# One step more of weight decoding among the attention steps of a fused attention and MoE kernel

## The chip, the cores and the metric

One core of one Trainium2 chip. The metric is the device time of one execution in microseconds (us); of several runs the median is given. TensorE multiplies, VectorE and ScalarE work element by element, GpSimd does some of that too, and SyncE's queue (SP) issues the transfers.

## The reference, cut to what matters

```python
# q, k, v: (2, 12, 448, 64); 896 tokens of 768
scores = scale * np.matmul(q, k.transpose(0, 1, 3, 2))      # causal mask, softmax
attn = np.exp(scores) / (np.sum(...) + 1e-09)
x = np.matmul(attn, v)                                      # -> (896, 768)
h = np.maximum(np.maximum(x @ w1, x @ w2), x @ w3)          # 768 x 768 each
x = h @ w_out                                               # 768 x 768
g = s * np.maximum(x @ w_in, 0.0) ** 2 + b                  # 768 x 2048
out = g @ w_out2                                            # 2048 x 768
```

## The kernel before

Attention comes first: 24 heads in 12 pairs, in a hand-written pipeline of steps t = 0 to 27. `ORDER` lists for even and odd steps the operations by two-letter names: S scores, R maxima (L252), E exponentials (L260), T transposes of the probabilities (L309) and V their copies (L397), PV the product with v (L324), N1 and N2 the reciprocals of the sums (L401, L404), RT, RV, Q1, Q2 the way of these out: a transpose (L282), a copy `rows` (L285), a store `rcd` to DRAM (L288) and a spread load `rb` (L293). XM divides (L339, result `xf`), XO and XL split that into the x tiles on GpSimd. M works at the first MoE product (the early product), and W runs a step of weight decoding at the steps t that `STEPS` names.

The weights come as 56 raw tiles of 768 KB, 64-bit words that have to be turned into 32-bit floats, then split into a high and a low part, since a matmul pass keeps only part of a float's digits. So each product is three passes: `whi` with the high part of the activations, `whi` with their low part, and `wlo` with the high part. A tile's decoding has four stages, one a step, and a new tile enters at every second call (`now[0] % 2`):

1. enter: ScalarE `wa` (L133) and `wr` (L134) read the raw tile;
2. clamps: VectorE L137, L140;
3. rounding: VectorE L146 and L151; between them `fetch_w` puts the load of another raw tile on SP's queue;
4. split: ScalarE `whi` (L156), VectorE `wlo` (L86).

So every call runs either the half "split of one tile, clamps of the next" or the half "rounding of one tile, enter of the next". In the MoE part there is one call per product. A product here is 18 matmuls of 448 columns (one 128-wide tile of weights, one half of the tokens); products are numbered from 0, the early one not counted: 0 to 34 use w1, w2, w3, 35 to 46 w_out, 47 to 78 w_in (two products per weight tile). The output stage (L559) follows: 2 halves of 16 calls of 21 matmuls of 384 columns, accumulated in seven PSUM tiles `m` for the seven blocks of tokens. `m` has eight buffers (banks) in all, for products and accumulators alike.

The evacuation of product k is queued with `after` and runs in the calls that follow: for w_in the Relu (L544) at call k + 1; at k + 2 VectorE's L533, which reads the bank for the last time, and on ScalarE L536 and L539 (`g`); at k + 3 VectorE's L86 (`g`, the low part). A call runs due evacuations first, the older ahead of the younger, and decoding behind them. The engines wait for each other only where data or buffers demand it; each works off its own queue in order.

```python
        for fns in [s.pop(0) for s in stages]:
            for fn in fns:
                fn()
        if not (enter and raws) or now[0] % 2:
            return
...
            acc = [ps.tile([128, 512], F32, tag="m", name="m") for _ in range(NTT)]
```

Of the kernel before, what the change touches and what calls it, by code (L numbers as in the profile page):

```python
# [27 lines left out]
)  # L28


FETCH = 18
STEPS = (20, 21, 23, 24, 25, 27)
EARLY = {24: 2, 25: 2, 26: 1, 27: 1}


# [8 lines left out]
def kernel(  # L44
# [55 lines left out]
    def begin(enter=True):  # L100
        for _, fn in sorted(due.pop(now[0], []), key=lambda e: e[0]):
            fn()
        decode(enter)
        now[0] += 1
# [5 lines left out]
    def fetch_w():  # L110
        if w_src:
            src = w_src.pop(0)
            raw = wr_p.tile([128, DM], I64, tag="wraw", name="wraw")
            nc.sync.dma_start(out=raw, in_=src)
            raws.append(raw)
# [54 lines left out]
    def attention():  # L170
        with ExitStack() as c2:
# [208 lines left out]
            def emit(t):  # L380
# [47 lines left out]
                if t in EARLY:  # L428
                    ops["M"] = lambda: [next(first, None) for _ in range(EARLY[t])]
                ops["W"] = lambda: [begin() for at in STEPS if at == t]  # L430
                for n in ORDER[h]:
# [3 lines left out]
            for t in range(n_heads + 4):  # L435
                emit(t)
                if t == FETCH:
                    fetch_w()
# [187 lines left out]
```

## Time and profile before

| | |
|---|---|
| median of 3 runs | 561.89 us (560.36 to 564.05) |
| the profiled execution | 564.4 us, of it 562.4 from first to last instruction |
| TensorE busy | 540.3 us, 96% |
| VectorE busy | 349.3 us, 62% |
| ScalarE busy | 293.1 us, 52% |
| GpSimd busy | 47.6 us, 8% |
| mean granted clock of TensorE | 0.994 of full |

Busy shares are averages over stages with different limits, and overlapping matmuls count as busy; where TensorE is not full, one has to look at the stage. Times on the timeline are counted from the first instruction. `PEclk` in the windows is the granted clock of TensorE as a part of full speed.

### The profile page before, as it was taken

What the parts mean: (1) busy time and instruction counts of PE and PEld (TensorE: products, weight loads), DVE (VectorE), ACT (ScalarE), POOL (GpSimd) and SP (SyncE); (2) the same over time, 40 slices, a digit from 0 to 9 for tenths busy, and PEclk for the clock granted to TensorE, in tenths of its full rate; (3) what the DMA queues carried; (4) which work ended last, traced back from release to release, by engine and by line L of the source; (5) the groups of instructions that cost most, each with busy time, mean ns of one, the idle gap of its engine ahead of it and who ended that gap; (6) DMA issues with size and microseconds to landing.
All of it is one profiled execution on the core that took longest, in us unless ns stands there. A gap on an engine that the chain in (4) does not pass through costs nothing.

```text
span 562.4 us, 7508 instructions
## 1 busy us (share of the span) xinstructions
PE 540.3 (96%) x2789; PEld 459.5 (82%) x2789; DVE 349.3 (62%) x653; ACT 293.1 (52%) x574; POOL 47.6 (8%) x43
## 2 busy tenths in 40 slices
PE   8999999989999999999999999888989799999997
PEld 4566665648999999999999997776768799999997
DVE  3555656676666676767666566575756677537501
ACT  2677777774335344344444575757666564334201
POOL 3125343222000000000000000000000000000000
PEclk9999999989999999999999999999999899999999
DMA  8768697523333333332323331313223144344102
GB/s 216 202 175 235 177 226 202 158 90 114 112 113 112 113 113 112 111 107 86 117 99 108 106 106 64 112 57 112 65 104 111 59 146 145 113 148 165 57 0 99
DMA packets 21108, 68.43 MB, mean 122 GB/s; under 512 B 3088, under 2 KB 9744, under 8 KB 21072
## 3 DMA queue, kind: packets, MB, share of 16 engines
q1 hardware_dynamic: 21072, 67.95, 38.6%
q8 instruction: 22, 0.36, 0.3%
q14 instruction: 14, 0.11, 0.1%
HBM read 55.05 MB, written 2.80 MB: 103 GB/s over the span
## 4 chain that ended last, share of the span: by engine, by line
PE 73%; ACT 16%; DVE 9%; issue 2%; ACTq 0%
PE m L453 31%; PE m L559 20%; PE s L244 9%; PE t L309 5%; PE o L324 5%; ACT r L536 4%; ACT g L539 3%; DVE wlo L86 3%; ACT r L544 2%; ACT whi L156 2%; ACT wa L133 2%; ACT wr L134 2%; PE warm L354 2%; DVE g L86 2%; DVE r L533 2%
## 5 line engine op out<-in xcount | busy, mean ns | idle before, releaser
L453 PE MATMUL m<-x,whi 128*128 128x448 f32 x816 | 233.8, 368 | 9.4 <-ACT whi L156 8.8
L453 PEld LDWEIGHTS m<-x,whi 128*128 128x128 f32 x816 | 152.5, 188 | 27.0 <-ACT whi L156 12.8
L453 PE MATMUL m<-x,wlo 128*128 128x448 f32 x408 | 150.8, 370 | 3.5 <-DVE wlo L86 3.5
L86 DVE TENSOR_TENSOR wlo<-wa,whi 128x768 fp32r<-128x768 f32 x56 | 53.6, 958 | 105.8 <-ACT whi L156 105.8
L559 PE MATMUL m<-whi,g 128*128 128x384 f32 x448 | 115.3, 337 | 2.6 <-DVE r L533 1.8
L453 PEld LDWEIGHTS m<-x,wlo 128*128 128x128 f32 x408 | 76.9, 188 | 14.0 <-DVE wlo L86 7.9
L559 PEld LDWEIGHTS m<-whi,g 128*128 128x128 f32 x448 | 81.9, 190 | 3.3 <-DVE r L533 2.2
L559 PE MATMUL m<-wlo,g 128*128 128x384 f32 x224 | 75.6, 338 | 0.5 <-DVE wlo L86 0.5
L133 ACT ACTIVATE wa<-wraw 128x768 f32<-128x768 f32 x56 | 51.0, 911 | 31.2 <-DMA wraw<-in_w_dram 25.2
L252 DVE CUSTOM_DVE_ANT_0 s<-s,mask 112x224 f32<-112x224 f32 (+1 forms) x96 | 43.7, 456 | 32.9 <-PE s L244 32.0
L156 ACT CAST whi<-wa 128x768 fp32r<-128x768 f32 x56 | 46.6, 831 | 32.1 <-PE m L559 16.4
L260 ACT ACTIVATE P<-s,mx 112x224 f32<-112x224 f32 (+1 forms) x96 | 46.8, 493 | 23.6 <-DVE mx L252 19.9
L151 DVE CUSTOM_DVE_ANT_0 wa<-wa,wr 128x1536 uint16<-128x1536 uint16 x56 | 54.7, 977 | 1.9
L146 DVE SCALAR_TENSOR_TENSOR wa<-wraw,wa 128x768 int32<-128x768 int32 x56 | 53.4, 954 | 0.5
L536 ACT ACTIVATE r<-r,sb 128x448 f32<-128x448 f32 x32 | 24.3, 758 | 51.1 <-DVE r L533 51.1
L134 ACT ACTIVATE wr<-wraw 128x768 int32<-128x768 uint32 x56 | 50.3, 899 | 0.0
L559 PEld LDWEIGHTS m<-wlo,g 128*128 128x128 f32 x224 | 42.5, 190 | 0.8 <-DVE wlo L86 0.8
L453 PE MATMUL m<-h,whi 128*128 128x448 f32 x144 | 40.9, 365 | 0.0
L244 PE MATMUL s<-HL 64*112 64x224 f32 (+3 forms) x112 | 39.4, 387 | 0.0
L397 ACT COPY PT<-t 112x336 f32<-112x336 f32 (+1 forms) x72 | 31.4, 476 | 11.1 <-PE t L309 11.1
L140 DVE TENSOR_SCALAR wa<-wa 128x768 int32<-128x768 int32 x56 | 33.0, 590 | 1.9
L309 PE MATMUL t<-ident,P 112*112 112x112 f32 x240 | 32.8, 268 | 0.1
(48 smaller groups left out, 486.7 us busy)
## 6 DMA issues: line engine op xcount, KB each, us to landing
wraw<-in_w_dram SPq DMA_DIRECT2D x56, 768.0 KB
QK<-HL SPq DMA_DIRECT2D x44, 224.0 KB
R<-in_qk_dram SPq DMA_DIRECT2D x11, 448.0 KB
V<-in_v_dram SPq DMA_DIRECT2D x12, 224.0 KB
rb<-rcd SPq DMA_DIRECT2D x24, 112.0 KB
out_dram<-o SPq DMA_DIRECT2D x14, 192.0 KB
R<-in_qk_dram SPq DMA_DIRECT2D x2, 224.0 KB
rcd<-rows SPq DMA_DIRECT2D x12, 3.5 KB
```

What stands on the lines that cost most here:

```text
L86: eng.tensor_tensor(out=lo, in0=full, in1=hi.bitcast(F32), op=ALU.subtract)
L133: nc.scalar.activation(out=f, in_=high.bitcast(F32), func=ACTF.Abs)
L134: nc.scalar.activation(out=r, in_=low.bitcast(U32), func=ACTF.Copy, scale=2.0 ** -29)
L146: nc.vector.scalar_tensor_tensor(out=a, in0=high, scalar=-0x40000000, in1=a, op0=ALU.bitwise_and, op1=ALU.bitwise_or,)
L151: nc.vector.tensor_tensor(out=a, in0=a, in1=r, op=ALU.add)
L156: nc.scalar.copy(out=hi, in_=f)
L244: nc.tensor.matmul(ps[:, o:o + n], lhsT, rhs, start=(m == 0), stop=(m == len(terms) - 1))
L260: nc.scalar.activation(out=s_t["P"][:, poff[i]:poff[i] + n], in_=ps[:, o:o + n], func=ACTF.Exp, bias=s_t["mx"][:, i:i + 1], scale=-1.0, ac ...
L309: nc.tensor.transpose(ps[0:CH, o:o + CH], head[t]["P"][:, a:a + CH], ident[0:CH, 0:CH])
L453: nc.tensor.matmul(p, wt[w][:, ws], cols(act[i], a, b), start=(i == 0 and n == 0), stop=(i == len(act) - 1 and n == 2),)
L536: nc.scalar.activation(out=r, in_=r, func=ACTF.Identity, scale=sb[:, 0:1], bias=sb[:, 1:2])
L559: nc.tensor.matmul(acc[t][:, 0:EH], gt[f][:, a, ts], w[:, ws], start=(f == 0 and n == 0), stop=(f == KG - 1 and n == 2),)
```

## The change

```diff
-FETCH = 18
-STEPS = (20, 21, 23, 24, 25, 27)
+FETCH = 17
+STEPS = (19, 20, 21, 23, 24, 25, 27)
 EARLY = {24: 2, 25: 2, 26: 1, 27: 1}
```

The first two raw tiles are requested behind attention step 17 in place of 18, and there are seven calls of the decoding among the attention steps in place of six. All later calls follow, so each stage of each tile is queued one call earlier, and in the MoE part the two halves change places between even and odd calls. What the attention steps run:

| step | before | now |
|---|---|---|
| 19 | | enter 0 |
| 20 | enter 0 | clamps 0 |
| 21 | clamps 0 | rounding 0, enter 1 |
| 23 | rounding 0, enter 1 | split 0, clamps 1 |
| 24 | split 0, clamps 1 | rounding 1, enter 2 |
| 25 | rounding 1, enter 2 | split 1, clamps 2 |
| 27 | split 1, clamps 2 | rounding 2, enter 3 |

VectorE, end of attention step 23 and step 24, before (`s,mx` are the maxima, `su` the sums, `rows` their copy):

```order
L252 ISA s,mx<-s,mask 112x448
L252 ISA mx 112x1
L146 SCALAR_TENSOR_TENSOR wa<-wraw,wa 128x768
L151 ISA wa<-wa,wr 128x1536
L401 TENSOR_SCALAR su<-su 112x8
L404 RECIPROCAL su<-su 112x8
L285 COPY rows<-t 8x112
L86 TENSOR_TENSOR wlo<-wa,whi 128x768
L137 TENSOR_SCALAR wa<-wa 128x768
L140 TENSOR_SCALAR wa<-wa 128x768
```

and with the change:

```order
L252 ISA s,mx<-s,mask 112x448
L252 ISA mx 112x1
L86 TENSOR_TENSOR wlo<-wa,whi 128x768
L137 TENSOR_SCALAR wa<-wa 128x768
L140 TENSOR_SCALAR wa<-wa 128x768
L401 TENSOR_SCALAR su<-su 112x8
L404 RECIPROCAL su<-su 112x8
L285 COPY rows<-t 8x112
L146 SCALAR_TENSOR_TENSOR wa<-wraw,wa 128x768
L151 ISA wa<-wa,wr 128x1536
```

The split and the clamps now stand ahead of the reciprocals, and the rounding behind the copy of the sums.

VectorE, from the last evacuation of w_out (`x_2857`, an x tile) into the first of w_in, before:

```order
L86 TENSOR_TENSOR x_2857<-m,x_2857 128x448
L146 SCALAR_TENSOR_TENSOR wa<-wraw,wa 128x768
L151 ISA wa<-wa,wr 128x1536
L533 SCALAR_TENSOR_TENSOR r<-m,r 128x448
L86 TENSOR_TENSOR wlo<-wa,whi 128x768
L137 TENSOR_SCALAR wa<-wa 128x768
L140 TENSOR_SCALAR wa<-wa 128x768
L86 TENSOR_TENSOR g<-r,g 128x448
L533 SCALAR_TENSOR_TENSOR r<-m,r 128x448
```

and with the change (the same tile has another number):

```order
L86 TENSOR_TENSOR x_2863<-m,x_2863 128x448
L86 TENSOR_TENSOR wlo<-wa,whi 128x768
L137 TENSOR_SCALAR wa<-wa 128x768
L140 TENSOR_SCALAR wa<-wa 128x768
L533 SCALAR_TENSOR_TENSOR r<-m,r 128x448
L146 SCALAR_TENSOR_TENSOR wa<-wraw,wa 128x768
L151 ISA wa<-wa,wr 128x1536
L86 TENSOR_TENSOR g<-r,g 128x448
L533 SCALAR_TENSOR_TENSOR r<-m,r 128x448
```

The first L533 (product 47) now stands behind the split and the clamps, the second (product 48) behind the rounding; so it goes on for all odd and even products.

SP's queue, from attention step 22 on (`rcd` and `rb` carry the sums, `wraw` is a raw weight tile), as one piece of the difference:

```order
-L288 DMA rcd<-rows 8x112
-L293 DMA rb<-rcd 64x448 x2
 L114 DMA wraw<-in_w_dram 128x768
 L288 DMA rcd<-rows 8x112
 L293 DMA rb<-rcd 64x448 x2
-L114 DMA wraw<-in_w_dram 128x768 x49
+L288 DMA rcd<-rows 8x112
+L114 DMA wraw<-in_w_dram 128x768
+L293 DMA rb<-rcd 64x448 x2
+L114 DMA wraw<-in_w_dram 128x768 x48
```

A load of a raw tile now stands between the last store of sums and the last spread load.

## Rows read from the trace of the kernel before

**Rows 1.** Windows; engines' busy us, granted clock, DMA share, GB/s.

```profile
131.50:303.20 171.70, 171.69 (x847) 159.16 (x848) 118.14 (x166) 75.31 (x105) 1.34 (x1) 1.00 0.32 108
...
345.00:437.00 92.00, 80.87 (x371) 67.72 (x369) 59.54 (x91) 59.73 (x95) 0.00 (x0) 1.00 0.27 92
```

**Rows 2.** Waits from 303 to 444 us: total, times, longest.

```profile
ACT r L536 <- DVE r L533: 47.9, 16, 3.2
...
PE m L453 <- ACT whi L156: 7.7, 10, 0.8
...
ACT r L544 <- PE m L453: 2.4, 1, 2.4
...
PE m L559 <- DVE r L533: 1.8, 1, 1.8
```

**Rows 3.** Timelines, ScalarE, then VectorE, at the end of w_in.

```profile
436.29 0.54 ACT L544 ACTIVATE r<-m 128x448 f32<-128x448 f32 x1
436.73 0.82 ACT L156 CAST whi<-wa 128x768 fp32r<-128x768 f32 x1
...
434.01 0.62 DVE L533 SCALAR_TENSOR_TENSOR r<-m,r 128x448 f32<-128x448 f32 x1
437.58 0.96 DVE L86 TENSOR_TENSOR wlo<-wa,whi 128x768 fp32r<-128x768 f32 x1 [2.94 <-ACT whi L156]
438.45 0.55 DVE L137 TENSOR_SCALAR wa<-wa 128x768 f32<-128x768 f32 x1
439.04 0.56 DVE L140 TENSOR_SCALAR wa<-wa 128x768 int32<-128x768 int32 x1
439.51 0.62 DVE L86 TENSOR_TENSOR g<-r,g 128x448 fp32r<-128x448 f32 x1
440.05 0.62 DVE L533 SCALAR_TENSOR_TENSOR r<-m,r 128x448 f32<-128x448 f32 x1
...
442.98 0.62 DVE L533 SCALAR_TENSOR_TENSOR r<-m,r 128x448 f32<-128x448 f32 x1
```

**Rows 4.** Timelines, ScalarE and VectorE, at the start of w_in.

```profile
306.92 0.55 ACT L544 ACTIVATE r<-m 128x448 f32<-128x448 f32 x1 [2.38 <-PE m L453]
...
308.90 0.62 DVE L533 SCALAR_TENSOR_TENSOR r<-m,r 128x448 f32<-128x448 f32 x1
...
317.51 0.62 DVE L533 SCALAR_TENSOR_TENSOR r<-m,r 128x448 f32<-128x448 f32 x1
```

**Rows 5.** Timeline of TensorE at the start of the output stage.

```profile
437.60 0.45 PE L559 MATMUL m<-whi,g 128*128 128x384 f32 x1 [0.79 <-ACT whi L156]
...
443.65 0.44 PE L559 MATMUL m<-whi,g 128*128 128x384 f32 x1 [1.85 <-DVE r L533]
```

**Rows 6.** A window just behind that wait.

```profile
444.00:446.00 2.00, 2.00 (x8) 2.00 (x7) 0.00 (x0) 1.97 (x5) 0.00 (x0) 0.50 0.48 194
```

**Rows 7.** The seam, steps 22 to 27: timelines, and one window.

```profile
111.84 0.52 DVE L252 CUSTOM_DVE_ANT_0 s<-s,mask 112x336 f32<-112x336 f32 x1 [0.44 <-PE s L244]
...
118.55 1.78 DVE L151 CUSTOM_DVE_ANT_0 wa<-wa,wr 128x1536 uint16<-128x1536 uint16 x1
...
129.56 0.62 DVE L339 TENSOR_TENSOR xf<-o,rb 128x448 f32<-128x448 f32 x1 [2.61 <-PE o L324]
...
119.38 0.95 ACT L133 ACTIVATE wa<-wraw 128x768 f32<-128x768 f32 x1
...
120.71 0.26 PE L282 MATMUL t<-ident,su 112*8 112x112 f32 x1 [0.86 <-DVE su L404]
...
122.32 0.67 PE L453 MATMUL m<-x,whi 128*128 128x448 f32 x2 [1.07 <-ACT whi L156]
...
125.11 1.66 PE L324 MATMUL o<-PT,V 112*64 112x448 f32 x4
...
131.51 0.68 PE L453 MATMUL m<-x,whi 128*128 128x448 f32 x2 [0.62 <-ACT t L462]
...
124.00:126.00 2.00, 2.00 (x8) 0.81 (x6) 1.97 (x4) 1.04 (x2) 1.05 (x1) 0.50 0.31 115
```

## The prediction

> **What bounds the kernel now.** I read the windows first, then the waits of the stage in which TensorE is not full, then the timelines of that stage's two ends, and last the seam between attention and MoE. The windows [rows 1] split the MoE part: from 131.5 to 303.2 us TensorE is busy 171.69 of 171.70 us, so nothing that ScalarE or VectorE do there is on the path; from 345 to 437 us it is busy 80.87 of 92.00 us. Between lies the start of the 32 products of the second MoE's first matrix (47 to 78 in the numbering above). The waits from 303 to 444 us [rows 2] show what rules there: ScalarE waits 47.9 us for `r L533` on VectorE, TensorE waits 7.7 us for `whi`, but ScalarE waits for TensorE once, 2.4 us, at the very start. From then on ScalarE and VectorE turn a closed loop that TensorE does not enter. A turn is two steps: from one even product's L533 to the odd one's is 442.98 - 440.05 = 2.93 us, from the odd one's at 434.01 to the next even one's 6.04 us, 8.97 us together [rows 3]. TensorE at full clock needs less: 171.7 us hold 847 matmuls, 0.203 us each [rows 1], so 36 take 7.3 us. It runs ahead on its stock of weight tiles, uses that stock up, and then stands at each new tile, ten times [rows 2].
>
> The stage does not end when the last weight tile is ready. The output stage takes seven of the eight banks of `m`, its last one is the bank of product 77, and that bank comes free with product 77's L533. TensorE begins at 437.60 us, gets through six accumulators and then stands 1.85 us, until 443.65, for L533 [rows 5], which VectorE began at 442.98 [rows 3]. From there it is busy to the end. So the end is set by one VectorE instruction, L533 of product 77, and about 119 us of matmuls and output behind it.
>
> **The change part by part.** *Weights one product further ahead.* This moves the waits for weights in the w_in stage, and nothing else there: TensorE's stock lasts one product longer, so I expect about seven waits for `whi` in place of ten. But evacuation of 32 products and all decoding still have to go through the loop up to product 77's L533, and no step of evacuation has moved. TensorE will arrive at the output stage about half a turn (4.5 us) earlier and stand for the banks of products 76 and 77 that much longer: the 1.85 us grow to some 5.5 us at the last bank (6.04 - 0.5 for the accumulator between) and about 2 us at the one before. Worth on the path: 0.
>
> *The decode halves change places in the loop.* Each step now holds the other half of the decoding (the second pair of order fences). Before, product 47 ended, its Relu ran at 306.92 us and L533 followed at 308.90 [rows 4], since the step between had only the rounding half, whose VectorE work was already under way. Now that step holds `whi`, `wlo` and the two clamps, and L533 stands behind them. Step by step with the steady rows [rows 3]: Relu to `whi` 0.44 (436.29 to 436.73), `whi` to `wlo` 0.85, `wlo` to L137 0.87, L137 to L140 0.59, L140 to the next 0.47: 3.22, so L533 of product 47 comes at 310.14 in place of 308.90, +1.24. From product 47 to 49 it took 317.51 - 308.90 = 8.61 [rows 4]; now it is the short gap and the long one, 8.97: +0.36. From 49 to 77 there are 14 full turns either way. Product 77's L533 thus comes **1.60 us later**. It is on the path, with no cover.
>
> *The start of the decoding in the attention steps.* The extra step 19 issues only ScalarE's `wa` and `wr`; the clamps move to step 20, the rounding to 21, `whi`, `wlo` to 23. In step 21 VectorE now runs L146 and L151 where it ran the clamps. Beside GpSimd's work L151 took 1.78 us [rows 7]; the step's two instructions so take 2.8 us. Against that stand the clamps removed from this place, and 0.44 us in which VectorE waited for TensorE afterwards [rows 7]. From below, cost 0 (all cover); from above 0.8, if every step passes it on; I take 0.1, since the chain through the next maxima has slack and TensorE's own queue sets the pace of attention.
>
> *The seam.* Before, VectorE finished L151 and went to N1 and N2 (L401, L404), TensorE's transpose of the sums started at 120.71, and the early product stood 1.07 us for `whi` at 122.32 [rows 7]. Now `whi` takes the place of `wa` on ScalarE, 119.38 us plus the 0.1, and the wait for it is gone. But VectorE has `wlo` and both clamps ahead of N1 and N2 (first pair of fences): `whi` at 119.5, and by the same steps as above 0.85 + 0.87 + 0.59 + 0.47 = 2.78 to L401, some 0.4 for L401 and L404 and the signal: the transpose at 122.7, **2.0 us later** than 120.71. The early product follows it after 0.5 us at 123.2, 0.9 later than 122.32. Its first six matmuls then no longer stand between `whi` and `wlo`; at the half clock that this stretch had (0.50 from 124 to 126 us [rows 7]) they need 6 x 2 x 0.203 = 2.4 us and end at 125.6, where the next product of attention began at 125.11 [rows 7]. **+0.5**, and as much for the first whole MoE product, at 131.51 before [rows 7], the 0.1 included. Bounds: -1.1, if the wait of 1.07 vanishes and the transpose costs nothing, and +2.0, if the transpose's delay goes through whole.
>
> *The transfers.* The two fetches stand one attention step earlier on SP, ahead of a store of sums; a fetch now also stands between the last store of sums and the last `rb`. The last divide (L339) stood 2.61 us for TensorE, not for `rb`, and began at 129.56 [rows 7]; that is the cover. I take 0; past the cover it costs what the `rb` is late.
>
> *TensorE's clock.* After the wait at 443.65 the granted clock is 0.50, that is 1.2 of 2.4 GHz, from 444 to 446 us, with 8 matmuls in 2 us [rows 6]; TensorE had stood three times in the 6 us before. Two us at half clock lose 1.0 us; the drop may outlast the window, so I put one drop at 1.6 us, an estimate. A longer wait may give the same drop again (0) or a second one (+1.6). I take 0, as the drop is already paid for.
>
> Sum: 1.60 + 0.5 = **+2.1 us**. The profiled execution took 564.4 us (span 562.4), 2.5 above the median of the runs; set against its own time the changed kernel would take 566.5, and set against the median of 561.89, **564.0 us**.
>
> **A rule that speaks for the change.** The trace shows ten waits for `whi` in 92 us of the stage [rows 2]. The Trainium skill, Perfetto Trace Analysis, section Optimization Strategy, says to look for the gaps on the engine that should be full, find what they wait for, and make that start sooner; by that rule the sum would be rival A's below, by the rows it is +2.1. The same section takes a gap that repeats as a possible sign of too little SBUF or PSUM. The repeating gaps here end with `whi`, but the one that ends the stage does end with a bank [rows 5], and in that the trace agrees.
>
> **The rivals.** *A, the waits go and nothing takes their place.* The output stage then begins half a turn earlier, 4.5 us, and the seam's 1.1 us go too: 561.89 - 5.6 = 556.3. If the drop of the clock at the output stage goes with the wait, 1.6 more. For it speaks that the wait at the last bank is the smallest of the stage, 1.85 us; against it, that product 77's L533 is two steps behind the weights in VectorE's queue and nothing in the change moves it up. Without the seam's part it is 557.4.
>
> *B, the seam turns into a stall.* VectorE stands for `whi` with N1, N2, the rows copy and the next rounding queued behind it; TensorE waits for N2, and behind it the store of sums, the fetch and `rb`. If the 2.0 us go through whole, the half clock lasts one drop longer (1.6) and `rb` comes 2 us after its cover, the price is 5.6 on top of 1.6: 569.1, slower. It decides when the last `rb` lands after about 131 us, so that the last x tile is late for the first product. Before, the window from 124 to 126 us holds 2 us x 115 GB/s = 230 KB [rows 7], which is `rb`'s two halves of 112 KB: they landed by 126. The transpose's 2 us and a tile of 768 KB ahead, 4 us at the 194 GB/s of the window in which one lands [rows 6], make 132 at the latest; most of that overlaps, so I expect some 130 and no price.
>
> *C, the change doesn't do what it says* can be left out: the rows of both orders show each half moved by one step through the whole MoE part.
>
> **How the numbers follow.** Forecast (the end waits for a bank, +2.1): 0.80; A: 0.10, nearly half of it past 1%; B: 0.10, mostly past 1%. A measurement of this kernel tells about 1% from no change, 5.6 us. The forecast's own bounds: 1.6 - 1.1 = +0.5 to 1.6 + 0.8 + 2.0 + 1.6 = +6.0 at the worst of all; runs differ by about 1.9 us to either side (560.36 to 564.05), so I take 560.5 to 567.5, which leaves out A and B. Faster by over 1%: 0.04; within 1%: 0.87; slower by over 1%: 0.09.
>
> **What would show it.** Right: the wait of L559 for L533 grows from 1.85 to over 4 us; TensorE begins L559 earlier but resumes at 445 or later; waits for `whi` in the stage fall to about seven; L533 of product 77 follows a long gap; the transpose L282 of step 24 waits 2 us longer for L404. Wrong: L559 begins 4 us earlier and runs without such a wait (A), or the first MoE product begins after 134 us (B). The forecast also fails if attention itself stretches: ScalarE's `wa` of step 19 would then wait for its raw tile and hold the exponentials behind it.

## The result and the profile after

| | before | changed |
|---|---|---|
| median | 560.36 us (558.63 to 564.05, 13 runs) | 564.02 us (562.34 to 570.44, 13 runs) |
| the profiled execution | 564.4 us, span 562.4 | 562.34 us, span 560.3 |
| mean granted clock in it | 0.994 | 0.991 |

The ratio is 1.0072 [1.0043, 1.0101]: some 4.0 us (2.4 to 5.7) slower, inside the band of 1%, which the interval's upper end just touches. Ratios, and medians that are split by clock below, leave out executions more than 1.5% above the fastest of their kernel. The forecast of 564.0 us is met, but the profiled executions stand the other way round: the one of the changed kernel is the fastest of its 13 runs, the one of the kernel before was slower than all 13 runs of before. So spans can't be set against each other, and the stages have to be.

**The stage of the 32 products, windows of the changed kernel** (columns as in [rows 1]):

```profile
131.50:303.20 171.70, 171.70 (x849) 159.14 (x848) 116.98 (x166) 75.52 (x108) 0.00 (x0) 1.00 0.32 110
345.00:437.00 92.00, 79.69 (x368) 67.22 (x366) 59.93 (x91) 59.74 (x95) 0.00 (x0) 0.99 0.28 94
```

Up to 303 us TensorE is full as before; in the later stretch it does no more than before, 368 matmuls in 92 us beside 371 [rows 1]. **The waits from 303 to 444 us:**

```profile
ACT r L536 <- DVE r L533: 50.0, 16, 3.2
...
PE m L559 <- DVE r L533: 7.0, 2, 4.8
PE m L453 <- ACT whi L156: 5.6, 7, 0.8
...
ACT r L544 <- PE m L453: 1.5, 1, 1.5
```

Against [rows 2] the waits for weights fell from ten to seven (7.7 to 5.6 us), those of the output stage for a bank rose from 1.8 to 7.0 us, and the loop of ScalarE and VectorE is unbroken. **TensorE at the start of the output stage** shows where the waits went:

```profile
429.04 0.45 PE L559 MATMUL m<-whi,g 128*128 128x384 f32 x1 [0.81 <-ACT whi L156]
...
435.09 0.54 PE L559 MATMUL m<-whi,g 128*128 128x384 f32 x1 [2.14 <-DVE r L533]
...
441.11 0.69 PE L559 MATMUL m<-whi,g 128*128 128x384 f32 x1 [4.83 <-DVE r L533]
```

It begins 12.1 us ahead of the last wait's end, before it was 6.05 [rows 5]. **VectorE at both ends of the stage**, with the Relu of product 47 on ScalarE in a fence of its own:

```profile
305.99 0.62 DVE L533 SCALAR_TENSOR_TENSOR r<-m,r 128x448 f32<-128x448 f32 x1
...
314.96 0.62 DVE L533 SCALAR_TENSOR_TENSOR r<-m,r 128x448 f32<-128x448 f32 x1
...
434.42 0.62 DVE L533 SCALAR_TENSOR_TENSOR r<-m,r 128x448 f32<-128x448 f32 x1
437.96 0.96 DVE L86 TENSOR_TENSOR wlo<-wa,whi 128x768 fp32r<-128x768 f32 x1 [2.92 <-ACT whi L156]
...
440.44 0.62 DVE L533 SCALAR_TENSOR_TENSOR r<-m,r 128x448 f32<-128x448 f32 x1
```

```profile
302.75 0.55 ACT L544 ACTIVATE r<-m 128x448 f32<-128x448 f32 x1 [1.50 <-PE m L453]
```

L533 of product 77 (440.44) now follows the long gap of 6.02 us; before it followed the short one of 2.93 [rows 3]. From the Relu of product 47 to it are 137.69 us; before 442.98 - 306.92 = 136.06 [rows 3, 4].

**The clock behind the wait, windows** (as [rows 6]):

```profile
440.00:442.00 2.00, 0.89 (x3) 0.89 (x4) 1.97 (x4) 0.88 (x2) 0.00 (x0) 0.50 0.00 0
442.00:444.00 2.00, 2.00 (x8) 2.00 (x7) 1.98 (x3) 2.00 (x4) 0.00 (x0) 0.50 0.50 135
444.00:446.00 2.00, 2.00 (x9) 2.00 (x8) 0.00 (x0) 1.97 (x4) 0.00 (x0) 0.62 0.65 258
446.00:448.00 2.00, 2.00 (x13) 2.00 (x13) 1.45 (x3) 0.97 (x2) 0.00 (x0) 1.00 0.00 0
```

TensorE, back from the wait at 441.11 us, runs at half clock up to about 445, as before behind its shorter wait.

**The seam, timelines of TensorE, VectorE and ScalarE** (as [rows 7]):

```profile
90.53 0.26 PE L282 MATMUL t<-ident,su 112*8 112x112 f32 x1
...
119.15 0.26 PE L282 MATMUL t<-ident,su 112*8 112x112 f32 x1 [2.83 <-DVE su L404]
...
119.46 0.65 PE L453 MATMUL m<-x,whi 128*128 128x448 f32 x2
...
127.34 0.68 PE L453 MATMUL m<-x,whi 128*128 128x448 f32 x2 [1.39 <-ACT t L462]
```

```profile
116.75 0.96 DVE L86 TENSOR_TENSOR wlo<-wa,whi 128x768 fp32r<-128x768 f32 x1 [2.62 <-ACT whi L156]
...
118.69 0.16 DVE L401 TENSOR_SCALAR su<-su 112x8 f32<-112x8 f32 x1
...
126.07 0.62 DVE L339 TENSOR_TENSOR xf<-o,rb 128x448 f32<-128x448 f32 x1 [0.50 <-PE m L453]
```

```profile
125.18 0.91 ACT L133 ACTIVATE wa<-wraw 128x768 f32<-128x768 f32 x1 [2.75 <-DMA wraw<-in_w_dram]
125.99 0.89 ACT L134 ACTIVATE wr<-wraw 128x768 int32<-128x768 uint32 x1
126.77 0.53 ACT L462 COPY t<-m 128x448 f32<-128x448 f32 x1
```

The first row, the transpose of step 18, runs ahead of the first moved call, and I count from it: it stood at 94.16 us in the profile before, so that execution was 3.6 us late where the change had moved nothing but two requests. In the fourteen profiles taken here that transpose lies anywhere from 90.35 to 94.16 us. The early product no longer waits for `whi`; instead the transpose of step 24 waits 2.83 us for the reciprocals, which stand behind `wlo` and the clamps. New is the end of the seam: `wa` waits 2.75 us for its raw tile, the copy `t`, which frees the early product, is queued behind it, and the first whole product, the one behind the early one, waits 1.39 us for that copy.

Stage by stage, in us from that transpose on. "Again" are two more executions, one of each kernel, from the last part of the experiments:

| | before | before again | changed | changed again |
|---|---|---|---|---|
| to the first whole product | 37.35 | 35.90 | 36.81 | 37.58 |
| from it to the Relu of product 47 | 175.41 | 175.42 | 175.41 | 175.42 |
| from there to L533 of product 77 | 136.06 | 136.13 | 137.69 | 137.74 |
| from there to the end | 119.42 | 117.89 | 119.86 | 119.14 |
| sum | 468.24 | 465.34 | 469.77 | 469.88 |

Against the profile before the change costs 1.5 us, against the second one 4.4. The ratio says 4.0. Which of the two executions of before stands for its runs is therefore the question that the experiments end with.

### The profile page after: what moved, and what is told of

Same layout as the page of the kernel before. It is cut to its first block, busy times and chain, and to the rows that moved or that the text cites. A ratio compares the mean times of both kernels' runs of the same rounds, so it can differ in the third digit from the quotient of the medians.

```text
span 560.3 us, 7507 instructions
## 1 busy us (share of the span) xinstructions
PE 534.4 (95%) x2788; PEld 457.8 (82%) x2789; DVE 348.1 (62%) x653; ACT 292.4 (52%) x574; POOL 47.2 (8%) x43
## 4 chain that ended last, share of the span: by engine, by line
PE 71%; ACT 17%; DVE 8%; issue 2%; DMA 1%; SPq 0%; ACTq 0%
PE m L453 31%; PE m L559 21%; PE s L244 9%; PE t L309 5%; PE o L324 4%; ACT r L536 4%; ACT g L539 3%; DVE wlo L86 3%; ACT r L544 2%; ACT wa L133 2%; ACT wr L134 2%; ACT whi L156 2%; DVE g L86 2%; DVE r L533 2%; DVE wa L137 1%
## 5 line engine op out<-in xcount | busy, mean ns | idle before, releaser
L559 PE MATMUL m<-whi,g 128*128 128x384 f32 x448 | 116.7, 340 | 7.8 <-DVE r L533 7.0
L244 PE MATMUL s<-HL 64*112 64x224 f32 (+3 forms) x112 | 37.6, 364 | 0.2 <-DVE HL L86 0.2
L244 PE MATMUL s<-QK 128*112 128x224 f32 (+1 forms) x88 | 32.7, 371 | 0.0
```

Of the source, the lines that this page charges most:

```text
L244: nc.tensor.matmul(ps[:, o:o + n], lhsT, rhs, start=(m == 0), stop=(m == len(terms) - 1))
L559: nc.tensor.matmul(acc[t][:, 0:EH], gt[f][:, a, ts], w[:, ws], start=(f == 0 and n == 0), stop=(f == KG - 1 and n == 2),)
```

## The experiments

The theory: the end is set by L533 of product 77; the swapped halves make it 1.6 us later, and weights that are ready sooner only lengthen the wait for its bank. The rivals are those of the prediction: the waits for weights were on the path (A), or the loss is the seam's (B). Times are medians; the ratio is to the kernel before, run beside each group.

**1. The loop alone.** The attention steps up to 25 stay as before, and the extra call runs in step 27.

```diff
-STEPS = (20, 21, 23, 24, 25, 27)
+STEPS = (20, 21, 23, 24, 25, 27, 27)
```

> The seventh call stands at the end of attention step 27, so attention up to there is as before and only the MoE part is one call ahead, its halves swapped. Theory (the end waits for the bank of product 77, whose L533 comes 1.6 us later by the swapped halves): +1.6 us against before, up to +3.2 with a longer drop of the clock, and a wait for L533 in the output stage of 4 us or more. Rival A (weights ahead are worth half a turn, and the change lost that in the seam): -4.5 us. Rival B (the loss is the seam's): 0.

567.56 us, 1.006 [1.0027, 1.0093]. From the Relu to L533 of product 77 it took 137.77 us, the changed kernel's figure, and TensorE stood for banks as there:

```profile
441.63 0.44 PE L559 MATMUL m<-whi,g 128*128 128x384 f32 x1 [2.14 <-DVE r L533]
447.66 0.69 PE L559 MATMUL m<-whi,g 128*128 128x384 f32 x1 [5.23 <-DVE r L533]
```

With the weights a product ahead and the first six calls where they were, nothing is won; A falls, and the loss is there without the 2 us at the transposes. But the run is not the loop alone. At the seam the extra call puts `wa` ahead of the copy `t`:

```profile
129.00 1.12 PE L453 MATMUL m<-x,whi 128*128 128x448 f32 x2 [2.37 <-ACT t L462]
```

This first whole product comes 38.65 us behind the transpose of step 18 and starts at half clock (0.50 from 130 to 132 us), and from it to the Relu it took 180.22 us in place of 175.4, most of the difference from matmuls that follow less closely on each other (the last section). So the 1.6 us of the loop are shown by the rows of the stage, not by this ratio.

**2. The seam alone.** All of the change among the attention steps, but the first call of the MoE part leaves its decoding to the next, so that the halves stand as before.

```diff
-        decode(enter)
+        if now[0] != len(STEPS):
+            decode(enter)
```

(with the parity counted by calls of `decode`.)

> The attention part is the changed kernel's, and the decoding of the first MoE call is left out, so the MoE part has the order of before. Theory: the seam is worth -0.5 to +0.5 us against before (in the changed kernel's profile the transpose came 2.07 us later and the first whole product 0.54 us earlier), the wait at the last bank stays at 1.85 us. Rival B: the whole loss of 3.7 us stands here. Rival A: 3.7 + 4.5 = 8 us of loss stand here.

565.36 us, 0.9983 [0.9954, 1.0011]. The wait at the last bank is the one before, 1.81 us, and L533 of product 77 follows the Relu after 136.19 us. The first whole product comes 37.59 us behind the transpose of step 18, as in the changed kernel run again. By the ratio the early attention calls thus cost between 2.6 us less and 0.6 us more than nothing, beside runs of before that had a mean granted clock of 0.994 at the median; B falls as the main loss. The profile holds some 3.4 us between the first whole product and the Relu (178.85 us in place of 175.4) whose cause was not found (the last section).

**3. Two calls more,** from step 18 on, with the requests at step 16: the halves stand as before, the weights are a whole turn ahead.

```diff
-FETCH = 18
-STEPS = (20, 21, 23, 24, 25, 27)
+FETCH = 16
+STEPS = (18, 19, 20, 21, 23, 24, 25, 27)
```

> Eight calls in attention (steps 18 to 27, fetch behind 16): weights two products ahead, the halves in the order of before. Theory: L533 of product 77 as early as before, the loop's +1.6 us gone; the seam has w0 ready two steps early, so -1 to +1 us against before; the output stage begins some 9 us earlier than before and stands that much longer for banks. Rival A: -4.5 us a step, -9 us. Rival B (more decoding in attention costs): +4 us or more.

568.62 us, 1.0054 [1.0019, 1.0089]. The loop did as expected, 136.2 us from the Relu to L533 of product 77, and TensorE stood four times for banks, 8.9 us:

```profile
315.42 0.55 ACT L544 ACTIVATE r<-m 128x448 f32<-128x448 f32 x1 [2.38 <-PE m L453]
```

```profile
451.62 0.62 DVE L533 SCALAR_TENSOR_TENSOR r<-m,r 128x448 f32<-128x448 f32 x1
```

The time did not: about 3 us slower. TensorE's timeline in attention, and two windows:

```profile
97.55 0.33 PE L244 MATMUL s<-QK 128*112 128x224 f32 x1 [1.53 <-DMA QK<-HL]
```

```profile
96.00:102.00 6.00, 4.47 (x21) 2.80 (x20) 3.89 (x11) 2.79 (x10) 1.88 (x2) 0.68 0.53 134
102.00:108.00 6.00, 6.00 (x21) 3.37 (x19) 3.75 (x10) 3.92 (x9) 0.00 (x0) 0.50 0.36 80
```

TensorE waited 1.53 us for a transfer of attention, and the granted clock was 0.50 from 102 to 132 us. This execution is the longest of the 12 and has the lowest mean clock, 0.958; the others had 0.973 to 0.982, so the window shows more than most of them lost. The two requests went out at 84.00 us, ahead of the `QK` requests at 86.22, and the DMA engines were over 0.9 busy from 84 to 96 us; in run 1 the two stand behind the `QK` requests, at 91.26, and TensorE did not wait there. That the one delayed the other fits, but was not tested by itself. A call may so cost through attention what it can't win behind it.

**4 and 5. More room ahead of the bank.** Both kernels with the first half of the output stage in another order: for its first two calls the token blocks 0 to 4 alone, then blocks 5 and 6 of both, so that the last bank is wanted later.

```diff
+LATE = {
+    0: [(0, t) for t in range(5)],
+    1: [(1, t) for t in range(5)] + [(f, t) for t in (5, 6) for f in range(2)],
+}
...
-                for t in range(NTT):
...
+                todo = LATE.get(f) if eh == 0 else None
+                for g, t in todo or [(f, t) for t in range(NTT)]:
+                    part(g, t)
```

> The kernel before, with the output stage's first half in another order: rows of tokens 0 to 4 for the first two calls, then rows 5 and 6 for both. The last bank is wanted 18 matmuls (3.1 us) later. Theory (the bank is what the end waits for): the wait of 1.85 us goes, and with it the drop of the clock: -1.9 to -3.5 us against before. Rival (something else holds the end, for example the next weight tile): 0, with the wait moved.

> The changed kernel with the output stage's first half reordered as in e4: rows of tokens 0 to 4 for two calls, then rows 5 and 6. In the changed kernel TensorE had done 18 matmuls before it stood for the bank of product 77; now it has done 36, 3.1 us more. Theory: the time from L533 of product 77 to the end falls from 119.9 to about 116.5 us (e4: 117.4, before: 119.4), and the weights ahead now show: against before -1 to +1 us, where the changed kernel had +4. Rival (the weight tile is what the output stage waits for): no gain over the changed kernel.

Before with it: 564.59 us, 1.0007 [0.9969, 1.0045]; its wait for L533 is gone, and 0.60 us for the second weight tile stand in its place. The changed kernel with it: 561.36 us, 0.999 [0.9963, 1.0017], beside 1.0055 [1.0023, 1.0087] for the changed kernel in the same group. One wait is left:

```profile
443.68 0.69 PE L562 MATMUL m<-whi,g 128*128 128x384 f32 x1 [4.53 <-DVE r L537]
```

From L533 of product 77 (here L537) to the end it takes 116.0 us in place of 119.86 and 119.14. So wanting the bank later gives the changed kernel some 3 us and the kernel before nothing that the runs show (117.4 us behind that L533 in place of 119.42 and 117.89). Between the two reordered kernels the early weights are worth 1.4 us behind the bank (116.0 and 117.4), just what the swapped halves cost ahead of it: from the Relu to the end it is 253.7 us in both. The times, 0.999 and 1.0007 of before, show no difference either.

**6 and 7. The loop taken apart.** ScalarE's `whi` is queued ahead of the evacuations that are due, `wlo` stays behind them; in the kernel before, and in the changed one.

```diff
     def begin(enter=True):
+        for s in stages:
+            if len(s) == 1:
+                s[0].pop(0)()
         for _, fn in sorted(due.pop(now[0], []), key=lambda e: e[0]):
...
-        stages.append([[clamped], [rounded], [split]])
+        stages.append([[clamped], [rounded], [split_high, split_low]])
```

> The kernel before, with one instruction moved: in the split step ScalarE does whi first, ahead of the due evacuations, and VectorE's wlo stays where it was. Theory (a closed loop of ScalarE and VectorE sets the pace of w_in, each standing 3 us a turn for the other): with whi first, both queues fit into some 7.3 us a turn in place of 8.97, TensorE becomes the bound again, and up to 16 x 1.6 = 26 us go: 535 to 545 us against 560 to 564 before. Rival (the engines' own busy time sets the turn): 0 to -3 us.

> The changed kernel with whi first in the split step. Theory: once the loop is no longer the bound, neither the place of the halves nor the weights one product ahead matter on the path; within 2 us of e9, the rest being the seam. If weights ahead were worth something in themselves: 3 us or more faster than e9. If the swapped halves still cost: 1.6 us slower.

540.35 us, 0.9612 [0.9569, 0.9656], and 539.0 us, 0.9583 [0.9539, 0.9627] (6 and 4 runs): 22 to 23 us faster, and the change worth nothing beyond the spread. The waits from 303 to 444 us of the kernel before with `whi` first, and a window:

```profile
ACT r L543 <- DVE r L540: 23.3, 16, 1.5
```

```profile
345.00:410.00 65.00, 65.00 (x323) 60.22 (x322) 52.93 (x81) 51.31 (x81) 0.00 (x0) 1.00 0.32 110
```

The wait of ScalarE for L533 (here L540) halves from 47.9 us [rows 2], a turn takes 7.32 us in place of 8.97, from one `whi` to the next:

```profile
350.09 0.84 ACT L161 CAST whi<-wa 128x768 fp32r<-128x768 f32 x1
...
357.41 0.84 ACT L161 CAST whi<-wa 128x768 fp32r<-128x768 f32 x1
```

and TensorE is full, with no wait at the output stage. That is the theory's closed loop, shown by breaking it: no more work was done by either engine than before, one instruction of each split stands earlier in one queue.

**8 and 9. Both kernels again.** The changed kernel in the group of 5 to 7, the kernel before in the group of 10 to 12.

> The changed kernel once more, for a second profile beside these runs. Theory: L533 of product 77 again 137.7 us behind product 47's Relu (before: 136.1), two waits for L533 at the output stage; against before +1.6 to +4. If the excess over 1.6 is a drop of TensorE's clock in the seam, this profile shows one there, with a wait for the raw tile and for the copy t ahead of it; if the clock is full there, the excess is not the seam's.

> The kernel before against itself, for a second profile and as a test of the measurement: ratio 1.000 within 0.004, L533 of product 77 again 136.1 us behind product 47's Relu. If the first profile's late start (the transpose of step 18 at 94.2 us, in the other profiles at 90.4 to 92.3) is chance, it comes at 90 to 92 us here.

564.44 us, 1.0055 [1.0023, 1.0087], and 559.6 us, 0.999 [0.9958, 1.0023]. The second is the control: before against itself is no change. Its windows behind the last bank, where the profile before had 0.50 [rows 6] and TensorE had stood 1.82 us up to 439.78:

```profile
440.00:442.00 2.00, 2.00 (x13) 2.00 (x13) 0.00 (x0) 1.97 (x5) 0.00 (x0) 1.00 0.66 277
442.00:444.00 2.00, 2.00 (x13) 2.00 (x13) 1.34 (x2) 0.62 (x1) 0.00 (x0) 1.00 0.00 0
```

The clock stays full there and at the seam as well, and the two missing drops are the 1.53 and 1.45 us by which it is shorter in the table. Over the 99 timed executions of the kernel before in these groups, 41 had a mean granted clock of 0.996 or more (median 559.45 us) and 58 one of 0.994 or less (563.17 us); only 13 reached 0.999. Of the 25 of the changed kernel none was above 0.991. The profile with two drops had 0.994 and the one with none 1.000. So in some two fifths of its executions the kernel before loses less to the clock than in its profile, and the changed kernel in none of these.

**10 and 11. The reciprocals first.** The changed kernel with the call of step 23 moved behind the copy of the sums in step 24, so that N1 and N2 stand ahead of `wlo` and the clamps again; in 11 the call of step 27 moved behind attention too, so that `wa` stands behind the copy `t`.

```diff
-STEPS = (19, 20, 21, 23, 24, 25, 27)
+STEPS = (19, 20, 21, 24, 25, 27)
...
+                        def rv():
+                            pair[p - 1]["r"][1]()
+                            if t == 24:
+                                begin()
```

and in 11 besides

```diff
-STEPS = (19, 20, 21, 24, 25, 27)
+STEPS = (19, 20, 21, 24, 25)
...
             for _ in first:
                 pass
+            begin()
```

> The changed kernel with the call of attention step 23 moved into step 24, behind the copy of the sums: N1, N2 and rows now stand ahead of wlo and the clamps on VectorE; ScalarE's order stays. Theory (VectorE's wait for whi holds the transpose): the transpose L282 comes 26.5 us after that of step 18, as before, not 28.6, and waits under 1 us; the early product starts 2 us earlier. The first whole product still stands behind wa of tile 3 and its transfer, so I expect only 0.5 to 1.5 us of that to arrive. Rival: the first whole product comes as much earlier as the transpose, 2 us.

> As f1, and the last call of attention (step 27) moved behind the copy t of the early product, so that ScalarE copies it without waiting for raw tile 3. Theory: the first whole product comes 2.5 to 3.5 us earlier than in the changed kernel (37.6 us behind the transpose of step 18), the loop's +1.6 us stays; about 1 to 2 us faster than before. Rival (something else holds the first product): as f1.

564.38 us, 1.0079 [1.0047, 1.0112], and 563.86 us, 1.0065 [1.0031, 1.0099]: no gain, and a miss. The transposes did come early again (25.6 us from step 18's, before 26.55, changed 28.6). In 10 the first whole product then waits 2.93 us for the copy `t` behind `wa`. In 11 the last divide and the product behind it wait for something else; VectorE, TensorE and SP's queue:

```profile
125.91 0.62 DVE L339 TENSOR_TENSOR xf<-o,rb 128x448 f32<-128x448 f32 x1 [0.46 <-DMA rb<-rcd]
```

```profile
126.68 0.64 PE L459 MATMUL m<-x,whi 128*128 128x448 f32 x2 [2.15 <-DVE xf L339]
```

```profile
117.39 0.27 SPq L288 DMA_DIRECT2D rcd<-rows  x1
120.50 0.36 SPq L114 DMA_DIRECT2D wraw<-in_w_dram  x1
120.97 1.09 SPq L293 DMA_DIRECT2D rb<-rcd  x2
```

The store of the sums is issued at 117.39 us, but `rb` only 3.58 us later, where the second execution of before has 1.67 between them: the fetch ahead of it on SP goes out at 120.50, just as VectorE's rounding, the last reader of a raw tile, ends at 120.43. `rb` stands behind it in SP's queue. So in 11 the transfers, not the transposes, were the next thing late. The first whole product did come earlier, 36.27 us behind the transpose of step 18 in 10 and 35.50 in 11 (changed 36.81 and 37.58). But half clock followed behind the standing TensorE (0.66 from 128 to 132 us): from there to the Relu it took 176.97 and 176.93 us in place of 175.4, and behind L533 of product 77 120.5 and 120.65 in place of 119.86 and 119.14. What the moves won at the seam went there.

**12. The best version,** 7 with both moves of 11.

> e10 (whi first, weights one product ahead) with both moves of f2. Theory: TensorE is the bound from the seam to the end, so what the seam gives arrives whole: 2 to 3.5 us faster than e10's 539.0, 535.5 to 537 us. Rival: the same as e10.

543.76 us, 0.9705 [0.9655, 0.9755] (6 runs), slower than 7 was in its group: a miss. Its first whole product comes 35.81 us behind the transpose of step 18, earlier than in 7 (37.46), but as in 11 it stood, the last divide waiting 0.77 us for `rb`, and half clock followed (0.50 from 130 to 132 us):

```profile
129.90 1.03 PE L466 MATMUL m<-x,whi 128*128 128x448 f32 x2 [2.43 <-DVE xf L346]
```

From there to the Relu it took 180.36 us, in 6 and 7 175.42. The greater part of that lies in a stretch that the moves don't touch:

```profile
140.00:170.00 30.00, 30.00 (x147) 27.25 (x146) 20.13 (x29) 12.39 (x17) 0.00 (x0) 1.00 0.31 102
```

147 matmuls, where 6, 7 and both kernels have 149 or 150. What the moves are worth by themselves therefore stays open. Versions 6 and 7 are the fastest of all that were run; the two can't be told apart.

## Why the prediction was right, point by point

**The time: met by two errors that cancel.** 564.0 was 561.89, the median of three runs, and 2.1. Thirteen runs gave 560.36, 1.5 less, and the change cost 4.0 by the ratio (3.7 by the medians), 1.6 to 1.9 more. That 564.02 was measured is luck; that the mechanism held, as told below, is not. The upper end of the range, 567.5, is not what its bounds add up to (561.89 + 6.0 + 1.9 = 569.8).

**What bounds the kernel: right.** The end goes with L533 of product 77. Runs 1 to 3 part the weights from the halves: with both moved that L533 comes after 137.77 us, with neither after 136.19, and with the weights ahead and the halves as before after 136.20. The halves alone decide when it comes, the weights only how long TensorE stands ahead of it. Runs 6 and 7 show the loop to be the cause of the whole stage's idle time. One reading was short: in the view of [rows 2] ScalarE waits for TensorE twice, not once, but both at the start:

```profile
ACT x L519 <- PE m L453: 1.5, 1, 1.5
```

**Weights, worth 0: right.** Seven waits in place of ten, as forecast; about 2 and 5.5 us at the last two banks forecast, 2.14 and 4.83 measured, 2.13 and 5.22 when run again. TensorE went on at 441.11, which is 444.7 on the time axis of the profile before; 445 or later was forecast. The Trainium skill, Perfetto Trace Analysis, section Optimization Strategy, asks to make start sooner what a gap waits for. Followed from the gaps' own label, that is this change, and gave no gain; followed one step further, to what `whi` itself stands behind, it gave run 6.

**The halves, 1.60 us: right.** 1.63 in the profile after, 1.71 in run 1; of it Relu to L533 of product 47 took 3.24 us against 3.22 worked out. No term was better known, since every gap in it had its row.

**Attention, 0.1: right.** The transposes of steps 18 and 22 lie 18.1 us apart, before 18.0.

**The seam, +0.5: the size was off, and its inside.** The transpose came 2.07 us later from step 18's (2.0 forecast) and the early product 0.77 (0.9). Most of the 2 us did not arrive: with full clock in both, the early product's last matmul began 35.06 us behind step 18's transpose, in the second execution of before 34.91. What the term left out came behind it: `wa` of step 27, which waits for its tile with the copy `t` behind it, and the wait for `t` of 1.39 us in place of 0.62. In the changed kernel run again that wait was 0.62 too, and the early product itself was late, at half clock (the last window of this text). Against the profile before the first whole product came 0.54 us earlier and 0.23 later in the two executions; against the one with full clock 0.91 and 1.68 later.

**The transfers, 0: a step that failed in its working, not in its size.** The prediction had `rb` land at some 130 us and named the divide's wait for TensorE, up to 129.56, as the cover. The landing was right: 126.26 in the changed kernel run again, 129.9 on the time axis of the profile before. The cover was not a fixed thing: that divide was late because the matmuls ahead of it ran at half clock [rows 7], in that execution. In the second execution of before it comes 33.96 us after step 18's transpose in place of 35.40, and against that the changed kernel's, which waits 0.69 us for `rb` and comes after 35.74, is late by 1.8. In neither profile of the changed kernel did the first whole product wait for that divide; it waited for `t`, so no row shows a price. In 11 and 12 it did wait for it.

**The clock, 0, "already paid for": the term that was mis-sized.** It was paid in that execution, not in all. The drop behind the bank cost the profile before 1.53 us against an execution that had none, near the 1.6 of the estimate. The changed kernel had it both times, and ended 1.25 and 1.97 us later than the execution without. Since 41 of 99 executions of before had a higher mean clock than that profile, the drop is in part new. By the second execution of before the sum is 0.91 + 1.56 + 1.97 = 4.4 us, or 1.68 + 1.61 + 1.25 = 4.5, near what the runs have (4.0 and 3.1); in place of the forecast's 2.1 that is 0.4 to 1.2 more at the seam and 1.3 to 2.0 more at the output stage. The rows of one execution that had both drops had hidden most of it. How often either kernel drops is counted above; why before keeps its clock in some executions and not in others is open.

## What to carry to other kernels

Before inputs are pulled ahead, look for the last buffer or instruction that ends the stage: if it is not the input that the gaps name, the waits only move. Two engines that hand work to each other in order can bind a stage at 65% busy each, and there the order of one instruction was worth 22 us, the lead tried here nothing. And a cover read from one execution should be looked at in another, above all one that stands on a clock drop.

## What the runs showed of the hardware

At a granted clock of 1.00 the matmuls of the same code were not always equally close: 147 in 30 us in the profiles of runs 1, 2 and 12, 149 or 150 in the other kernels and executions where this was counted, 148 in run 3. It is 2%, some 3.4 us over the 175 us to the Relu (178.85 in run 2), nearly as much as the whole change. What sets it was not found.

The clock dropped in different places in executions of one kernel: at the seam the changed kernel had 1.00 from 120 to 124 us in one profile and 0.57 in the other,

```profile
120.00:124.00 4.00, 4.00 (x12) 1.96 (x11) 3.60 (x5) 1.34 (x3) 1.73 (x2) 0.57 0.59 182
```

with TensorE busy without a gap in both.
